# One attention, mixture and convolution program under a new table of step order and engine choices

## The chip, the cores and the metric

The kernel runs on one core of one Trainium2 chip. The metric is the device time of one execution in microseconds (us). Before the change the median of three runs is 481.59 us (481.58 to 484.25). A change of 1% is 4.8 us.

## The reference

Three blocks follow each other, for a batch of 4, a sequence of 448, 12 heads of 64 and a model width of 768:

```python
# 1. causal attention of 12 heads; x is its output, heads side by side: (4, 448, 768)
attn = softmax(mask(q @ k.T / 8));  x = attn @ v
# 2. four experts, each a causal attention head of its own; the two best by gate are mixed
logits = x @ w_gate
out += w_e * (softmax(mask((x @ wq[e]) @ (x @ wk[e]).T / 8)) @ (x @ wv[e]) @ wo[e])
# 3. feed-forward block: relu, a convolution of width 3 along the sequence, a sigmoid gate
h = relu(out @ w_in);  y = (h * sigmoid(conv3(h, conv_w))) @ w_out
```

All is computed to nearly full 32-bit accuracy. A matrix product is therefore done in three passes over operands that are split into a rounded high part and a remainder (`hi` and `lo` in the code).

## The kernel before, in words

The work is a list of tasks (`Program.add`), and each task has an engine or a choice of engines. A table in the source, `ORDER`, is a packed list of pairs (task, engine). `Program.run` walks through it and issues the tasks in that order, each on the engine named. So the table alone sets the order of the instructions on each engine's queue and decides, where there is a choice, which engine does a step. Nothing is decided at run time: an engine runs its own queue in order and waits at semaphores.

The stages, in the order of time:

- **Attention heads.** `A b_p` is the pair p of heads of batch b (24 pairs). For batches 1 to 3 the natural q and k (tile `nat`) are split into `sk_A` by `hi`, then `lo` for k and `lo` for q (lines 349, 347 or 353 for the high part on POOL, ACT or DVE; line 356 for the remainder on POOL or DVE). TensorE (PE) makes scores into one of three PSUM banks (line 673, or 630 for batch 0 without the split). DVE adds the mask and takes the row maximum (line 686, tiles `P_A` and `nm_A`), which also frees the bank for the next score. ACT takes the exponent (line 695), DVE the sum and its reciprocal (lines 703, 706, tile `r_A`), and one of ACT, POOL and DVE scales the rows (lines 347, 349, 353). PE transposes (line 726), ACT or DVE evacuates to `PT_A`, PE multiplies with v (line 797), and the result is split into `xT`.
- **Experts.** `M b_p` is the pair p of experts of batch b (8 pairs), with projections on PE at lines 991 and 1042 and the same softmax (`P_M`, `nm_M`).
- **Weights, woven into the first 300 us.** Weights arrive as 64-bit floats. `from_f64` turns them into 32-bit floats (`wm` for the input weight, `wom` for the output weight; ACT line 440, DVE lines 445 to 457), and `fold_piece` splits them into `whl` and multiplies them (line 918). `wout_convert` makes sums and differences of quarters of the output weight (tile `wom`, line 356) and splits each into `wohl`, `hi` on ACT or DVE and `lo` on POOL or DVE. These are stored to memory for the last stage.
- **Feed-forward.** Lines 1338 to 1369 make the hidden layer and its gate; line 1471 does the output product with a seven-product scheme over quarters; line 1517 adds the quarters up; the last stores end the kernel.

The functions that matter for the steps below are short:

```python
def copy(e, dst, src, scale=1.0, scale2=None):        # lines 345 to 353
    if e == "ACT": nc.scalar.activation(dst, src, AF.Copy, scale=scale)
    elif e == "POOL": nc.gpsimd.tensor_scalar(dst, src, ...)
    else: nc.vector.tensor_scalar(dst, src, ...)
def two(e, dst, a, b, op):                            # line 356
    (nc.gpsimd if e == "POOL" else nc.vector).tensor_tensor(dst, a, b, op)
th = add(either("whi", ...), 0, hi, need, take=[whl], ..., port=True)   # in wout_convert
tl = add(either("wlo", 0, of_two(n)), 0, lo, [th], ...)
```

A few small products of the identity matrix with itself (line 1587) are put in by `warm` where the table's planner saw PE idle for long.

Of the kernel before, what the change touches and what calls it, by code (L numbers as in the profile page):

```python
# [35 lines left out]
    "xry9H9wXnQ!RRci4JAe@k$R*J=|Lut9mou_3)O={fDmXr8bEd-zaWFC1nM*L0+~aNqXtm-NDxYnMxpSiUy09%@39}S&xwB^#t=K$m&75|3~C<r"
    "0rd&RMo%DS5O%B!8^T^8chSR`bMyiF4n2WcM6IF@P^YLHlmJaZYtR<78x5e7=!fVB=p*zg8i`rM%wrC)N7yam5s`{HM=?sT(5zB%sj_s3ctb>z"
    "Mlm?dBIXvAM}aUbj1VKocrnwM6XFJD2XjZ<$KXMim~QkSnhNSgvq3bJ0Tl*~p(oJ8Xbt8Y@dxG<+gjRQI#xPgDg;fG1~6t!0@H!%EA7K{VfKi}"
    "m_tk!Gk{^CKqMTgwWy=0yXX~Bh>C&kF(@nzi^C3-Qb|LlY*J_G9Pur2h1f?LBTbMDrM6OU=>iET&4LC<o1`VuEP5WjgqD#&SQhppT7;b@nMpFx"
    "5NVaPP1+~rNi>Rr!lo>iPM5BgZkB2(dXkvrAtgwCMIMR_tHow19i%SOBTy#@#zXT4i$;njiU3NkC_^Ih=sXXvj|cEBu)UxhZvZq58sPcJ0rD;B"  # L40
    "taPumjS?W4DPKxIm0pzIm$vfSc{z}P5~FlcdMQ_>Aj%a9MZr;Su=iL{5wa*ren1{0Z;|ul_ryOytDsBL83{rrkSSyiSwJQf@pxjMk~am?^X5Q9"
    "lw&f2+)sH)nIKP-H$gj~N90cOQ}Q@vfxJXsCGUfF$a&Bi=o$GEL@VMHiHa0Ox*|)Fy9mNp@MkH@l)phBFcORh5Ajwh<Gd}(HigD#^A|u=u$IpT"
    "i@{3p9{HTy$&2x3cmn=4`6n642bIk8R(Njycght-LDrHzC4D8WB|ym^_EkHMAK>4Bbl_acJZ00qV^5VHQ1<P4yM_FT_kp*{JK&x2@D5yw8Eodq"
    "`2!{GC9_2fMaxC&MK`<`<gKFJA~*Oa1yKT}DyXeg3>8PEJLuG}_ALJy|1n?e;8MTYukCksup?Y_$m=Yjm5i6%@`g%~j(m~V(N2w(%#_F-z0|!T"
    "R*9(OwCJMfJ?$0P&f_^!Me`+Ehuxtov6Qqs9y@M|?u$HBfXXQr6|a=YO7avf^@P&K|He}k_wYyfkm4L)S8Of5pk7n|qDiP>@Fd?;94}trZ_qx`"
    "X81ty5+7AeEr!sLw0`PpiJ3~H$!QxUG3s{7LCI-JkK;4#nd6q)ft$p2QV&aTv~2OiVm57<dR~&Fb{0P^?!w`VZ%UpOKQEpJ-<AN58Qf8E(!s$C"
    "@k_XQu!bg}1@Z0pC9s9|vUsX^ruc2~9Cd}dQv8Pc1~*PUrd`r{aF9|&shjqYwg!&lH^KPQwc;2!L(78O!5@lOaWUEp#wg>3;}^#d+7x4svCcm&"
    "4$wCE>(pJU48KP`q7LGQaXZDIi!X}1z`fvS;G1F{9zsXb?~5V0ZSZICDDH%6!SC=ls4jdr4T0;Sb>eAsHeEp9#61V^;4X1raG!Asx|<%LYw3fu"
    "G1>$TkE7w%=@;~CI+&5c579R12XqcDPw&MK;6*qEPKW!4W8Cp4<8RuGW8SgkSaTp4X8J81M?a>Y;cjrZI0&AAr{d@EQ}~zo=lG9~-x({6cZ~n$"
    "e_(tCTX8NNfJ@;J_-)4l1H!yu#Oc?J1^gm@n|{j}1Fz$E@%xS}y`P?EP?>nfF$2lOF~9Kt$-j2|bikZchM1vY9D!L(wDT8S-f`lPF@(%E`niM4"  # L50
# [1601 lines left out]
```

## Time and profile before

| | before |
|---|---|
| median of 3 runs | 481.59 us (481.58 to 484.25) |
| profiled execution, own time | 482.01 us |
| its span, first to last instruction | 480.2 us |
| PE busy | 471.0 us (98%) |
| DVE, ACT, POOL busy | 392.9, 347.4, 333.1 us |
| DMA | 93.26 MB, mean 194 GB/s |

The profiled execution has 1.8 us outside of the span and lies 0.42 us over the median of the runs. Busy times are unions of an engine's instructions. PE's matmuls are pipelined, so its busy share says that it rarely stood still, not that it ran at its peak. Each view is one execution on the one core.

### The profile page before, as it was taken

What the parts mean: (1) busy time and instruction counts of PE and PEld (TensorE: products, weight loads), DVE (VectorE), ACT (ScalarE), POOL (GpSimd) and SP (SyncE); (2) the same over time, 40 slices, a digit from 0 to 9 for tenths busy, and PEclk for the clock granted to TensorE, in tenths of its full rate; (3) what the DMA queues carried; (4) which work ended last, traced back from release to release, by engine and by line L of the source; (5) the groups of instructions that cost most, each with busy time, mean ns of one, the idle gap of its engine ahead of it and who ended that gap; (6) DMA issues with size and microseconds to landing.
All of it is one profiled execution on the core that took longest, in us unless ns stands there. A gap on an engine that the chain in (4) does not pass through costs nothing.

```text
span 480.2 us, 9966 instructions
## 1 busy us (share of the span) xinstructions
PE 471.0 (98%) x3114; PEld 398.9 (83%) x3114; DVE 392.9 (82%) x1155; ACT 347.4 (72%) x965; POOL 333.1 (69%) x475
## 2 busy tenths in 40 slices
PE   8999999999899999999999999999999999999997
PEld 6667898988679888878988877888789999999996
DVE  4999999999999798998889893287878887968482
ACT  5999999999788789987889994268987445422000
POOL 4697899799787989986879896117486485641530
PEclk9999999999899999999999999999999999999999
DMA  7693769986675986856884846616666783752122
GB/s 220 207 211 110 209 181 239 277 268 169 193 230 158 265 258 184 201 179 185 259 212 120 197 156 202 286 72 235 205 226 219 257 308 125 242 212 76 40 77 96
DMA packets 45846, 93.26 MB, mean 194 GB/s; under 512 B 4833, under 2 KB 27233, under 8 KB 45793
## 3 DMA queue, kind: packets, MB, share of 16 engines
q1 hardware_dynamic: 45360, 92.28, 63.4%
q8 instruction: 24, 0.39, 0.3%
q10 hardware_dynamic: 432, 0.34, 0.2%
q14 instruction: 30, 0.24, 0.2%
HBM read 60.72 MB, written 25.69 MB: 180 GB/s over the span
## 4 chain that ended last, share of the span: by engine, by line
PE 85%; DVE 6%; POOL 4%; ACT 3%; issue 1%; DMA 1%; POOLq 0%; DVEq 0%; ACTq 0%
PE bank L1471 21%; PE bank L991 11%; PE bank L797 11%; PE bank L726 10%; PE bank L673 10%; PE bank L1338 8%; PE bank L1042 7%; PE bank L918 3%; PE bank L630 2%; DVE P_A L686 2%; ACT P_A L695 2%; PE bank L1587 1%; POOL P_M L349 1%; DVE wohl L353 1%; DMA wset<-wohl 1%
## 5 line engine op out<-in xcount | busy, mean ns | idle before, releaser
L695 ACT ACTIVATE P_A<-P_A,nm_A 112x224 f32<-112x224 f32 (+3 forms) x192 | 99.4, 521 | 9.4 <-DVE nm_A L686 8.8
L686 DVE CUSTOM_DVE_ANT_0 P_A<-bank,mask 112x448 f32<-112x448 f32 (+3 forms) x192 | 79.6, 440 | 10.0 <-PE bank L630 5.4
L356 POOL TENSOR_TENSOR sk_A<-nat,sk_A 64x448 fp32r<-64x448 f32 (+1 forms) x67 | 77.5, 1158 | 4.6 <-ACT sk_A L347 0.6
L991 PE MATMUL bank<-xT,wqk 128*128 128x448 f32 x288 | 66.9, 372 | 0.0
L726 PE MATMUL bank<-ident,P_A 112*112 112x112 f32 x480 | 61.2, 264 | 1.4 <-ACT PT_A L347 0.7
L349 POOL TENSOR_SCALAR P_A<-P_A,r_A 112x112 f32<-112x112 f32 (+3 forms) x95 | 48.4, 523 | 11.3 <-DVE r_A L706 9.6
L726 PEld LDWEIGHTS bank<-ident,P_A 112*112 112x112 f32 x480 | 48.9, 135 | 8.2 <-POOL P_A L349 1.7
L991 PEld LDWEIGHTS bank<-xT,wqk 128*128 128x128 f32 x288 | 51.7, 188 | 3.9 <-DVE nm_A L686 0.2
L673 PE MATMUL bank<-sk_A 128*112 128x224 f32 (+3 forms) x288 | 51.9, 305 | 0.2 <-DVE nm_A L686 0.2
L1359 DVE SCALAR_TENSOR_TENSOR bank<-h,cw,bank 128x448 f32<-128x448 f32 x64 | 42.6, 686 | 8.9 <-ACT bank L1357 7.4
L797 PE MATMUL bank<-PT_A,v 112*64 112x448 f32 (+3 forms) x384 | 49.9, 404 | 0.0
L347 ACT ACTIVATE P_A<-P_A,r_A 112x224 f32<-112x224 f32 (+3 forms) x94 | 46.3, 522 | 2.9 <-DVE r_A L706 1.6
L1471 PE MATMUL bank<-up,ws 128*128 128x448 f32 x198 | 46.7, 367 | 0.0
L347 ACT ACTIVATE PT_A<-bank 112x336 f32<-112x336 f32 (+1 forms) x94 | 42.0, 472 | 5.2 <-PE bank L726 4.8
L797 PEld LDWEIGHTS bank<-PT_A,v 112*64 112x64 f32 x384 | 25.5, 136 | 23.1 <-issue 11.5
L1471 PE MATMUL bank<-us,ws 128*128 128x448 f32 x180 | 44.3, 366 | 0.0
L673 PEld LDWEIGHTS bank<-sk_A 128*112 128x112 f32 x288 | 40.6, 175 | 4.1 <-issue 0.4
L1042 PE MATMUL bank<-wvg,xT 128*112 128x260 f32 x288 | 43.5, 290 | 0.0
L1471 PEld LDWEIGHTS bank<-up,ws 128*128 128x128 f32 x198 | 37.2, 188 | 3.3
L1042 PEld LDWEIGHTS bank<-wvg,xT 128*112 128x112 f32 x288 | 36.8, 175 | 2.3 <-issue 1.1
L349 POOL TENSOR_SCALAR P_M<-P_M,r_M,g_w 112x336 f32<-112x336 f32 (+3 forms) x63 | 36.1, 584 | 3.0 <-ACT PT_A L347 1.3
L695 ACT ACTIVATION_READ_ACCUMULATOR P_A<-P_A,nm_A 112x1 f32 x192 | 36.8, 192 | 0.0
(181 smaller groups left out, 1053.5 us busy)
## 6 DMA issues: line engine op xcount, KB each, us to landing
nat<-in_qk_dram SPq DMA_DIRECT2D x72, 224.0 KB, 4.0
ws<-wset SPq DMA_DIRECT2D x7, 1536.0 KB, 8.9
wset<-wohl SPq DMA_DIRECT2D x18, 512.0 KB, 4.5
g<-g SPq DMA_DIRECT2D x32, 224.0 KB, 2.6
wraw<-in_w_in_dram SPq DMA_DIRECT2D x12, 512.0 KB, 4.9
woraw<-in_w_out_dram SPq DMA_DIRECT2D x12, 512.0 KB, 4.9
v<-in_v_dram SPq DMA_DIRECT2D x24, 224.0 KB, 4.8
out_dram<-osb_c SPq DMA_DIRECT2D x21, 224.0 KB, 2.0
```

Source lines behind the costliest of these rows:

```text
L347: nc.scalar.activation(dst, src, AF.Copy, scale=scale)
L349: nc.gpsimd.tensor_scalar(dst, src, scale, 1.0 if scale2 is None else scale2, ALU.mult, ALU.mult)
L356: (nc.gpsimd if e == "POOL" else nc.vector).tensor_tensor(dst, a, b, op)
L673: nc.tensor.matmul(sp[:CP], t[:, j.o[h], m * CP : (m + 1) * CP], t[:, j.o[h] + k, :w], start=(k == 2), stop=(k == 1),)
L686: nc.vector.tensor_tensor_reduce(rows(i), st["s", i][:CP, :w], mask[:, S - w :], -SCALE, 3.0e38, ALU.add, ALU.min, st["nm"][:, i : i + 1],)
L695: nc.scalar.activation(rows(i), rows(i), AF.Exp, bias=st["nm"][:, i : i + 1], scale=-1.0, accum_out=st["sm"][:, i, 0:1],)
L726: nc.tensor.transpose(pt[:CP, o : o + CP], rows(i)[:, kt * CP : (kt + 1) * CP], ident[:CP, :CP])
L797: nc.tensor.matmul(st["ov"][h * D : (h + 1) * D, kt * CP : S], j.v[:, kt, h, :], j.PT[h][:, col_base[kt] : col_base[kt] + S - kt * CP], st ...
L991: nc.tensor.matmul(st["ps"][:, :S], proj["wqk"][:, a, cc, w, p * P : (p + 1) * P], xT[b, cc][:, b2, :], start=(cc == 0 and (a, b2) == PASS ...
L1042: nc.tensor.matmul(st[i][:CP, :VW], xT[b, cc][:, a, i * CP : (i + 1) * CP], proj["wvg"][:, b2, cc, :], start=(cc == 0 and (a, b2) == PASSE ...
L1359: nc.vector.scalar_tensor_tensor(y, h, w, y, ALU.mult, ALU.add)
L1471: nc.tensor.matmul(ps(pb)[:, :S], wset[s][:, a, m, c2 * P : (c2 + 1) * P], unit(operands[q, c2, name][0])[:, b2], start=(c2 == 0 and (a, b ...
```

## The change

Only the table `ORDER` is another one. The tasks, what they need, their buffers, the banks and all other lines are the same. The table decodes to another order of the same tasks and to other engines for some of the steps that have a choice.

```diff
 ORDER = (
-    "c-jrt$4}b{gD_xMa0ORz1y^tdS8&DMxPpH!xPwh*B_LS|NLB(ep9Ew+2}oAL<Xwr9l_*&$kU3E103-(>IRKdhkUd~B2TBeBascwK1Y}nFzUQxa"
...
+    "c-jTQM@-v`V*p@J@B~lr&jUQc6Fk8ayzvB2@WeKGm4KuYkW>QlDgk+wfTR*8tpp^M7^xJKcVN5&kQ{*I0OTEj^nl4b0LdXh4vc>##;ert!@$_E"
...
 )
```

Counted over the two programs, the steps that went to other engines in the first 300 us are these:

| step | DVE | ACT | POOL |
|---|---|---|---|
| `wohl` hi, 128x512 | 13 to 8 | 5 to 10 | |
| `wohl` hi, 128x256 | 4 to 0 | 2 to 6 | |
| `whl` hi, 128x512 | 1 to 1 | 2 to 7 | 9 to 4 |
| `whl` lo, 128x512 | 0 to 3 | | 12 to 9 |
| `sk_A` hi, 128x896 | 1 to 3 | 17 to 10 | 18 to 23 |
| `sk_A` lo of k, 128x448 | 2 to 8 | | 34 to 28 |

PE has the same products; only the identity products of line 1587 go from 17 to 19. SP issues the same 293 instructions. Three places show how the queues differ.

**Place 1, DVE, near the scores of the expert pair `M` 0_1** (`P_M_1_1`, `nm_M_1_1`) and the last head pairs of batch 1 (`P_A_5_1`, `P_A_5_0`). `wohl_1_2` is a split of the output weight. Rows of line 686 are the row maxima. Before:

```order
L829 TENSOR_TENSOR xT_3_1838<-bank_65,xT_3_1838 128x448
L353 TENSOR_SCALAR wohl_1_2_1860<-wom_1_0_1660 128x512
L356 TENSOR_TENSOR wohl_1_2_1860<-wom_1_0_1660,wohl_1_2_1860 128x512
L686 ISA P_M_1_1_1865,nm_M_1_1_1866<-bank_62,mask 112x224
...
L686 ISA P_M_1_1_1865,nm_M_1_1_1866<-bank_62,mask 112x112
...
L686 ISA P_M_1_1_1865,nm_M_1_1_1866<-bank_61,mask 112x448
...
L703 TENSOR_REDUCE r_A_5_0_1814<-sm_94 112x4
L706 RECIPROCAL r_A_5_0_1814<-r_A_5_0_1814 112x4
```

Now:

```order
L686 ISA P_A_5_1_1769,nm_A_5_1_1770<-bank_61,mask 112x336
...
L353 TENSOR_SCALAR wohl_1_2_1838<-wom_1_0_1638 128x512
L686 ISA P_A_5_0_1823,nm_A_5_0_1824<-bank_62,mask 112x448
...
L356 TENSOR_TENSOR wohl_1_2_1838<-wom_1_0_1638,wohl_1_2_1838 128x512
L703 TENSOR_REDUCE r_A_5_1_1771<-sm_92 112x4
L686 ISA P_A_5_0_1823,nm_A_5_0_1824<-bank_65,mask 112x224
...
L686 ISA P_A_5_0_1823,nm_A_5_0_1824<-bank_65,mask 112x112
...
L706 RECIPROCAL r_A_5_1_1771<-r_A_5_1_1771 112x4
```

The split stands one head earlier now, between row maxima of `A` 1_5, and its two halves are no longer next to each other.

**Place 2, POOL at the same place.** The `wom_1_0<-wom_1_0` step makes what the split `wohl_1_2` reads, so DVE's split waits for it. Before:

```order
L356 TENSOR_TENSOR wom_1_0_1660<-wom_1_0_1660 128x256
L349 TENSOR_SCALAR P_A_5_1_1720<-P_A_5_1_1720,r_A_5_1_1722 112x448
L356 TENSOR_TENSOR sk_A_1_1703<-nat_1_1_1704,sk_A_1_1703 128x448
L356 TENSOR_TENSOR sk_A_1_1768<-nat_1_0_1769,sk_A_1_1768 128x448
L349 TENSOR_SCALAR P_A_5_0_1812<-P_A_5_0_1812,r_A_5_0_1814 112x112
```

Now:

```order
L356 TENSOR_TENSOR wom_1_0_1638<-wom_1_0_1638 128x256
L356 TENSOR_TENSOR sk_A_1_1726<-nat_1_1_1727,sk_A_1_1726 128x448
L349 TENSOR_SCALAR P_A_4_0_1670<-P_A_4_0_1670,r_A_4_0_1672 112x336
L349 TENSOR_SCALAR P_A_5_1_1769<-P_A_5_1_1769,r_A_5_1_1771 112x448
L356 TENSOR_TENSOR sk_A_1_1726<-nat_1_1_1727,sk_A_1_1726 64x448
```

Before, three steps stood between the `wom` step and the first step that needs something from DVE's queue behind the split (`r_A_5_0`); now two do (the next needs `r_A_5_1`).

**Place 3, DVE near the head pair `A` 3_0** (`sk_A_0`, batch 3). Before:

```order
L686 ISA P_A_4_0_2863,nm_A_4_0_2864<-bank_61,mask 112x448
...
L353 TENSOR_SCALAR sk_A_0_2881<-nat_0_1_2882 128x2x448
L356 TENSOR_TENSOR wohl_1_2_2855<-wom_1_0_2544,wohl_1_2_2855 128x512
L353 TENSOR_SCALAR oc_0_2895<-bank_66 128x448
L703 TENSOR_REDUCE r_A_4_1_2834<-sm_88 112x4
```

Now:

```order
L356 TENSOR_TENSOR sk_A_4_2845<-nat_4_0_2846,sk_A_4_2845 64x448
L353 TENSOR_SCALAR sk_A_0_2873<-nat_0_1_2874 128x2x448
L356 TENSOR_TENSOR sk_A_0_2873<-nat_0_1_2874,sk_A_0_2873 128x448
L353 TENSOR_SCALAR wohl_1_2_2882<-wom_1_0_2605 128x512
L703 TENSOR_REDUCE r_A_5_0_2771<-sm_94 112x4
```

DVE has four such splits in a row where it had two.

## Rows read from the trace of the kernel before

**Rows 1.** The page: span, busy time by engine, the chain by engine.

```profile
span 480.2 us, 9966 instructions
PE 471.0 (98%) x3114; PEld 398.9 (83%) x3114; DVE 392.9 (82%) x1155; ACT 347.4 (72%) x965; POOL 333.1 (69%) x475
PE 85%; DVE 6%; POOL 4%; ACT 3%; issue 1%; DMA 1%; POOLq 0%; DVEq 0%; ACTq 0%
```

**Rows 2.** Windows of the span: busy time (instructions) by engine, granted clock, DMA.

```profile
core 0: us, PE busy (x) PEld busy (x) DVE busy (x) ACT busy (x) POOL busy (x), PEclk, DMA share, GB/s
12.00:120.00 108.00, 106.92 (x810) 86.50 (x812) 103.24 (x367) 105.49 (x321) 93.01 (x128) 1.00 0.75 208
120.00:132.00 12.00, 9.79 (x68) 7.52 (x65) 11.71 (x27) 8.80 (x25) 9.22 (x12) 0.86 0.65 192
132.00:288.00 156.00, 155.43 (x1176) 131.55 (x1175) 139.35 (x467) 137.25 (x411) 131.92 (x178) 1.00 0.71 200
288.00:420.00 132.00, 131.69 (x733) 113.73 (x732) 97.16 (x201) 80.53 (x176) 74.24 (x124) 1.00 0.62 216
```

**Rows 3.** Timeline around the stall: start, duration, engine, idle before and releaser.

```profile
123.85 0.65 POOL L349 TENSOR_SCALAR P_A<-P_A,r_A 112x448 f32<-112x448 f32 x1
123.91 3.05 DVE L353 TENSOR_SCALAR wohl<-wom 128x512 fp32r<-128x512 f32 x1 [0.22 <-POOL wom L356]
123.93 2.11 PE L797 MATMUL bank<-PT_M,vm 112*64 112x448 f32 x16
124.45 2.23 POOL L356 TENSOR_TENSOR sk_A<-nat,sk_A 128x448 fp32r<-128x448 f32 x2
127.60 0.38 DVE L686 CUSTOM_DVE_ANT_0 P_M<-bank,mask 112x224 f32<-112x224 f32 x1
127.77 0.67 ACT L440 ACTIVATE wm<-wraw 128x512 f32<-128x512 f32 x1 [2.69 <-issue]
128.24 0.90 PE L673 MATMUL bank<-sk_M 128*112 128x336 f32 x2 [2.21 <-DVE nm_M L686]
129.12 0.36 POOL L349 TENSOR_SCALAR P_A<-P_A,r_A 112x112 f32<-112x112 f32 x1 [2.44 <-DVE r_A L706]
```

**Rows 4.** Windows right behind the stall, columns as in rows 2.

```profile
128.30:130.00 1.70, 1.70 (x8) 1.50 (x9) 1.67 (x8) 1.70 (x6) 0.80 (x2) 0.50 0.83 269
130.00:132.00 2.00, 2.00 (x12) 1.79 (x11) 2.00 (x5) 2.00 (x6) 1.90 (x3) 0.59 0.97 271
```

**Rows 5.** Groups of one form: count, busy us, mean ns, idle before.

```profile
L353 DVE TENSOR_SCALAR wohl<-wom 128x512 fp32r<-128x512 f32 x13 | 10.6, 813 | 1.4 <-DMA wset<-wohl 1.2 <-POOL wom L356 0.2
L356 DVE TENSOR_TENSOR sk_A<-nat,sk_A 128x448 fp32r<-128x448 f32 x2 | 3.7, 1838 | 0.0
L356 DVE TENSOR_TENSOR sk_A<-nat,sk_A 64x448 fp32r<-64x448 f32 x3 | 2.0, 670 | 0.1
L356 POOL TENSOR_TENSOR sk_A<-nat,sk_A 128x448 fp32r<-128x448 f32 x34 | 39.2, 1155 | 2.0 <-ACT sk_A L347 0.6
L349 POOL TENSOR_SCALAR P_A<-P_A,r_A 112x336 f32<-112x336 f32 x23 | 14.0, 610 | 3.9 <-DVE r_A L706 3.4 <-DVE r_A L703 0.2
```

**Rows 6.** Timeline of one split that meets POOL and one that does not.

```profile
151.89 1.15 POOL L356 TENSOR_TENSOR sk_A<-nat,sk_A 64x448 fp32r<-64x448 f32 x1
151.93 1.59 DVE L356 TENSOR_TENSOR sk_A<-nat,sk_A 128x448 fp32r<-128x448 f32 x1
154.29 0.41 DVE L353 TENSOR_SCALAR wohl<-wom 128x512 fp32r<-128x512 f32 x1
155.79 0.74 POOL L356 TENSOR_TENSOR wom<-wom,wom 128x256 f32<-128x256 f32 x1 [2.74 <-DVE wohl L356]
```

**Rows 7.** Timeline of PE: transposes, scores, identity products.

```profile
120.74 1.12 PE L726 MATMUL bank<-ident,P_A 112*112 112x112 f32 x10
121.63 1.24 PE L673 MATMUL bank<-sk_M 128*112 128x448 f32 x6
5.50 2.27 PE L1587 MATMUL bank<-ident 128*128 128x128 f32 x18
```

More of the change, by code (lines that the diff above doesn't have):

```diff
@@ L36 @@
[L36 to L50, printed above, removed]
@@ L96 @@
[L96 to L98 removed]
+    "c-jTQM@-v`V*p@J@B~lr&jUQc6Fk8ayzvB2@WeKGm4KuYkW>QlDgk+wfTR*8tpp^M7^xJKcVN5&kQ{*I0OTEj^nl4b0LdXh4vc>##;ert!@$_E"
+    "Zdfl24;R9~@E6#Z*h%aYY%dl8&%oMY6!;*P1e3$GFh48;yM*1qOfU!R81@798a@wSf^Wlj;e)Ud*fi`V>@DmStgm38fCcX;5WpR91zZQWz}MiX"
+    "@C$ezegxly-@+#gK49svkJu&HDr^(B4cmw1VW0wJ0lr|mpsPSyFj6p95P(PFZSWp=AG`z3E!2aIpx+VVLM19!uvoBOATQJwiVA22oC0luvEZ`M"
@@ new lines @@
+    "Rp2Y|7e)#*g|UK6L3^RO&{c>>bQe+(gN4I|H-){0V8r_Z1mbhSmx9BB<ASq-yMl{?&)6Zj6O=8SEPP+cLhupGg=>gS#0Xr5&>*G@L4`g<9&v=o"
+    "!rv8c7H$>p7akOjAp4L5$T8$e;c4LxViGxxJVjg};s`gwf@nkZAchcqhy?Zl_91p3VMe{dzQf)ka>xZF5{W~CkRyl;svWh8+&~^70VE5lK)!)n"
+    "kXy)h#4hpx=|bVr-6$9c0Rp2D=nrUAA-)hO44`5t8Cr)FAzes6@(g)_yhEZ;U{o)Pg&sr=qkbjEke$d3vKyI2;ZZy2ee@}sf>xvXXcO9rp2Un`"
+    "CQ!HNafB7?z+Rvu=owTFwSrnl9inrXW$ZKJbK*<l2^zqxViqt=3<xuZnZ`^aW)MgW4nr^Hl!{9KKu}RElmL}Rx1*O)pHcg$6Vxe6fRSOYP`9Xc"
+    "%mFHh#e>?4e3(t*Ht~?SjoHIo5s{=@Vi4Vf9zu_!htW8a1JjE>!u-G-U_hi};tyhHk)pJ%biA~`6acY69i;-$E^!jwQ<N*6ES)a3V04%mrW2FF"
@@ new lines @@
+    "^keq1{YBlFK}=Vv9u)#bK-ZW%3<`_G4wep=g0TRJMN*Uaq=ix`={0eV_>Q<t>?h5W#z}*uVG<R)Ncuq3mp%e*khVycQg>;vl!cunWk4p<EINn&"
+    "gcf2K(W|8!rBbX0yH!f1xF{Kli!@F0kyc1CQWuCt@l*Jep`y{EPExi=PT3=AC@?OXOXSkHF0P;3&mH8pQ;d{hZWn2?$U_d2rJx8UPx?Vhl>Px)"
+    "0UcsbuxHqBrC&=kBrccF&2lHWeV{?m2q+8crhF-laIdgurFW$$3YgMI8KbmuJGeN?9Tr>^CqE#MlPAf@qD^w1yiFz)-IKnNu1OFwf_zcB0h%W-"
+    "lD9#7pkWHNh(Kl+vB`Y0g8Pc{j515naUr}%<j3R*&@_1t^pyOJEaz!>P9BoCL=hHIdGaD{5sQ}xb#YfHGu#~aGnYb^la0K;K_D;^Y%FpX;lTiy"
+    "1wI0ugM7RkWs{;I&x2egZ6*Gaj*?yS73e4Bnu6mUkwstyc!hjQz9gH-_mnNl0(XVG&fVvpaQVC_FT;DtyC*||KddX(4XYOXl-FNEECH2lTlcKl"
@@ L99 @@
+    "B!9-*l2ftHWP7kX_-pLf;Oo$ziM`lgv7TgqayGdU$H!T5S=^X#CZ^-L_-+!28{?UTCZ0>~#=pi*F;5KDN@%6FvRh|jzsC-f?zpzq+}f2GNC;Y$"
+    "t=EbB#M6W*4o%{c$mB`#EP0h&YaLA9CSk3v*3H(=)}Gd#)`tmZvcGk_HPDJmO|{Op0?BCWFRe%M^SCH^(t6f9-#XMPPia%n6XujF<%>Uvcf=Q4"
+    "qw!ekIu1?T#*vAU)@<Uc^{%xoMM#aOCKH{h{Z?60lk7=>Q+=u5QadSXik;d|9i~oFUGb;!?YJ@NPUc(vsngUyQd6nflpr;qT1<UNO()(Zd`Vma"
+    "NXXOL^nUs<ZBDz=3yJrMlk`UFHswzz((&Y3`ZE1@x-C7Po=VTA=hNT}BGZ}fN%yBAX+j2-re+q?8|e>ec7~ANN>kH==@)5XW+cT*i_@}<DdWiK"
+    "Gye}Cay~W"
 )
```

102 lines of the change are left out of this document (50 added, 52 removed).

## The prediction

> **What bounds the kernel now.** I read the page first: of a span of 480.2 us PE is busy for 471.0, and 85% of the chain that ended last is PE [rows 1]. The reader is to see that a new order can't win much by making another engine faster; it wins where PE stands still or crawls. So the second view is the table of windows [rows 2]. PE's idle time is 108.00 - 106.92 = 1.08 us in 12 to 120, 2.21 us in 120 to 132, 0.57 us in 132 to 288 and 0.31 us in 288 to 420. One window of 12 us holds more than the 396 us around it, and it alone shows a granted clock below 1 (0.86).
>
> The third view is the timeline of that window [rows 3]. DVE starts the high part of a weight split (`wohl`, line 353) at 123.91 and is done 3.05 us later. The same form takes 0.41 us where POOL runs nothing [rows 6], and 0.81 us in the mean of 13 [rows 5]. POOL runs a 0.65 us step from 123.85 and two of `sk_A` until 124.45 + 2.23 = 126.68; only then does DVE move. Its next row maxima of `P_M` begin at 127.60. PE had a batch of line 797 of 2.11 us from 123.93 to spend, then waits 2.21 us for exactly that DVE line (row of 128.24: released by DVE `nm_M`, line 686). POOL's later wait of 2.44 us and ACT's of 2.69 us end with the same release, so nobody was the next in line: all engines lost the time together. That is why I take it to be real loss and not a wait that covers another. After it the clock is granted at 0.50 and 0.59 in the next 1.70 and 2.00 us [rows 4], the lower level (1.2 GHz), right behind the pause.
>
> The other DVE splits show the same sort of meeting at smaller prices: 1.59 us for a remainder that began 0.04 us after a POOL step of 1.15 us [rows 6], and a mean of 1.84 us for the two of 128x448 against 0.67 us for the three of 64 partitions [rows 5]. None of these stopped PE for long, as the idle sums of the long windows say [rows 2].
>
> **The change, part by part.** Everything moves a little, so I cost the one place where PE lost time, then what is added, then the loads.
>
> *The stall goes from its place.* Now the split `wohl_1_2` stands on DVE between row maxima of `A` 1_5, its remainder one row maximum later, and the row maxima of `M` 0_1 follow well behind. What PE had lost is 2.21 us of idle [rows 3] and the slow clock: 1.70 x (1 - 0.50) + 2.00 x (1 - 0.59) = 0.85 + 0.82 = 1.67 us [rows 4]. Together -3.88 us.
>
> *It may come back smaller.* The split is still released by POOL's `wom` step, and POOL has two steps ready behind that one (`sk_A` of 1.16 us, `P_A` of 0.61 us, means of [rows 5]); the third needs a reciprocal that DVE makes behind the split. Taken as before, DVE would be held for up to 1.16 + 0.61 = 1.77 us instead of 126.68 - 123.91 = 2.77 us. What is late next is the row maximum of `A` 1_5_0 in bank 62, whose reader on PE comes after six transposes (six tenths of 1.12 us) and three scores of six matmuls (1.24 us), 1.9 us of cover [rows 7]. DVE's path from PE's last score is the split and the row maximum: 0.41 + 1.77 + some 0.6 = 2.8 us, the 0.6 estimated from the 0.38 us of a row maximum half as wide [rows 3]. The cost is between 0 (DVE comes when POOL is through) and 2.8 - 1.9 = 0.9 us. I take +0.5: the met remainder in rows 6 paid nearly all of POOL's step, so half of the full price is the middle, not the floor. Without a pause as long as 2.21 us I expect no slow clock; the shorter ones in the long windows have a granted clock of 1.00 [rows 2].
>
> *Two identity products more.* They are recorded as four; 18 took 2.27 us, so 0.50 us if PE had work, nothing if it was waiting [rows 7]. They stand where the planner sees PE idle: +0.2.
>
> *Loads.* DVE loses nine `wohl` halves and gains six `sk_A` remainders of k. At the met prices the six cost 6 x 1.84 = 11.0 us, at the unmet 6 x 0.67 = 4.0 us; the five large `wohl` alone gave back 5 x 0.81 = 4.1 us [rows 5]. So DVE is between even and 7 us heavier over the first 288 us, in which it is idle for 4.8 us in 12 to 120 and 16.7 us in 132 to 288 [rows 2]. POOL gives away six steps of 1.16 us (6.9 us), and more in its `whl` halves, and is idle for 15.0 us in 12 to 120. What POOL no longer does can't be met there. I cost the loads at 0 because PE is the bound, and their cover in 12 to 120 is thin on DVE (4.8 us) and on ACT (108.00 - 105.49 = 2.5 us): if it is gone, PE pays. In place 3 four splits stand in a row on DVE, but POOL's next steps wait for the last of them, so there is no step of POOL for it to meet. SP's loads and stores are the same in number; with DMA busy at 0.75 or less in the long windows [rows 2] I cost their new order at 0.
>
> By the Trainium skill, "SBUF — State Buffer", section "Who interferes with whom", DVE and GpSimd share a port pair as an exclusive lock, and whoever starts first holds it for the whole instruction while the other is blocked. By that rule alone the split would have been free when POOL's first step ended at 124.50, 0.59 us after it began. The trace disagrees in size: DVE stayed out over two more POOL steps, for 2.77 us. By the rule the return of the stall would cost at most 0.41 + 1.16 + 0.6 - 1.9 = 0.3 us, and the sum, with half of that in place of 0.5, would be 478.5 and not 478.8 us.
>
> *Sum.* The profiled execution's own time is 482.01 us, its span 480.2. 482.01 - 3.88 + 0.5 + 0.2 = 478.83. This execution lies 0.42 us over the median of the runs, so against 481.59 the forecast is **478.4 us**, 0.7% less.
>
> **The rivals.**
>
> *More comes back (faster by over 1%).* With all of POOL's relief and the new places, the small waits of PE go too: 3.88 + 1.08 + 0.57 + 0.31 = 5.84 us, no return and no extra products. 482.01 - 5.84 - 0.42 = 475.75 us. For it: those waits are mostly waits for the same three engines. Against it: a new order brings its own small waits, and the long windows were already at 99% and more. Chance 0.25.
>
> *The change doesn't do what it says: the stall only moves.* The split still follows POOL's `wom` step at once, and eight `wohl` halves of 128x512 and more `sk_A` steps are left on DVE. One stop of 3.88 us anywhere leaves 481.6 to 482 us. For it: the meeting in rows 6 shows that such meetings are common, and each needs only a second ready step of POOL to grow. Against it: only one meeting in 288 us grew to 3 us. Chance 0.18.
>
> *DVE's new splits hold up the row maxima (slower).* Three to four splits now stand in a row on DVE at three places of the attention stage, and six remainders of k came to DVE whose two kin took 1.84 us each. If POOL has two or more steps ready in each of these places, DVE is late by over the 2.11 us that a batch of line 797 covers; from there PE stops, and a stop with its slow clock cost 3.88 us. Three of them against the one that goes: 482.01 + 2 x 3.88 - 0.42 = 489.35 us. For it: the prices in rows 5. Against it: place 3 shows POOL waiting for DVE there. Chance 0.12.
>
> **How the numbers follow.** The forecast has the remaining 0.45, and its own range is 476.9 to 480.5: the return of the stall between 0 and 0.9 + 1.67 with the slow clock, the products between 0 and 0.5, and about 1 us for new small waits. The range that holds 8 in 10 takes in the faster rival to 474.5 and the moved stall to 484.5, and leaves out the slower rival and a little below. A change of 1%, 4.8 us, is about what a measurement of this kernel can tell from none. Faster by over 1% means under 476.8: the faster rival and a sliver of the forecast, 0.28. Slower means over 486.4: most of the slower rival, 0.10. Within 1%: 0.62.
>
> **What would show it.** In the changed profile no DVE step of line 353 or 356 before 300 us should last over 2.3 us, no window of 12 us between 12 and 288 should have over 1 us of PE idle, and the clock should be 1.00 in all of them. The split `wohl` near 125 us should show 0.4 to 2.2 us. POOL's busy time should be lower before 288 us, DVE's about the same. I am wrong if a PE wait of over 2 us for `nm_A` or `nm_M` stands elsewhere, if the clock falls again, or if PE's busy time itself grows in the long windows without a wait that stands out.

## The result: 0.9% slower, and the profile after

The changed kernel takes 486.52 us in the median of 4 runs (486.22 to 487.05), against 481.62 us for the kernel before. The ratio is 1.0092, with a 95% interval of 1.0071 to 1.0112. The forecast of 478.4 us has the wrong sign, and the range that was to hold 8 in 10, 474.5 to 484.5, ends 2 us too low. The profiled execution took 486.78 us, so the two traces are 486.78 - 482.01 = 4.77 us apart.

The first lines of the page after, which answer to [rows 1]: span, busy time by engine, and the shares of the chain that ended last.

```profile
span 484.9 us, 9943 instructions
PE 471.3 (97%) x3118; PEld 396.7 (82%) x3118; DVE 399.2 (82%) x1161; ACT 346.4 (71%) x971; POOL 324.5 (67%) x463
PE 61%; DVE 12%; POOL 10%; ACT 7%; DMA 4%; issue 4%; SPq 1%; DVEq 0%; POOLq 0%; ACTq 0%
```

PE's busy time is the same within 0.3 us, so PE was not given more work. But PE's share of the chain fell from 85% to 61%: the end now hangs on DVE, POOL, ACT and DMA as well. The windows, with the columns of [rows 2] and in answer to them, say where.

```profile
12.00:120.00 108.00, 105.18 (x799) 84.10 (x800) 100.53 (x356) 103.55 (x316) 94.96 (x130) 1.00 0.73 201
120.00:132.00 12.00, 11.12 (x91) 8.61 (x88) 11.36 (x40) 10.45 (x32) 9.26 (x11) 1.00 0.93 270
132.00:288.00 156.00, 152.78 (x1152) 129.72 (x1152) 136.04 (x464) 136.32 (x410) 118.05 (x165) 1.00 0.71 195
288.00:420.00 132.00, 130.44 (x730) 110.55 (x727) 104.00 (x210) 76.36 (x174) 69.13 (x119) 1.00 0.62 216
```

The stop in 120 to 132 is smaller, 0.88 us of PE idle for 2.21, and the granted clock there is 1.00 for 0.86. The three long windows, which had 1.96 us of PE idle together, have 2.82 + 3.22 + 1.56 = 7.60. What PE waits for, summed over the trace (columns: who waits, for whom, us in sum, times, longest):

```profile
PE bank L726 <- POOL P_M L349: 1.8, 2, 1.0
PE bank L726 <- DVE P_M L351: 1.4, 2, 0.9
PE bank L1587 <- POOL ident masks.py:199: 1.4, 1, 1.4
PE bank L726 <- DVE P_A L353: 1.1, 1, 1.1
PE bank L673 <- DVE nm_A L686: 0.9, 2, 0.5
PE bank L673 <- DMA sk_M<-sk_M: 0.8, 1, 0.8
PE bank L726 <- POOL P_A L349: 0.5, 1, 0.5
PE bank L1042 <- POOL wvg L356: 0.5, 1, 0.5
```

The row of 1.4 us for `ident` is the start of the kernel and is in both. The rest wait for POOL, DVE and a DMA queue, none over 1.1 us at a time (three more of 0.2 to 0.3 us are left out). Before, the same view had one wait of 2.2 us and nothing else over 0.5 us after the start.

Idle time alone leaves out matmuls that are drawn out. So I put the two traces side by side at equal matmul work: each TensorE step counts as long as steps of its kind take back to back (the lower quartile over both traces), the steps are summed in the order of their ends, and the moments are compared at which the two traces have done the same sum.

```
work done, us    before at    changed at    changed minus before
      70            86.2          86.4           +0.18
      80            96.4          98.0           +1.61
     100           116.9         118.9           +1.99
     110           131.9         131.2           -0.75
     180           206.0         206.1           +0.11
     200           227.6         229.5           +1.91
     290           322.8         324.3           +1.56
     300           332.7         336.1           +3.37
     350           385.7         389.7           +3.96
     370           405.8         410.3           +4.54
     end           476.6         481.2           +4.55
```

So 2.74 us were won at the old stop and 7.3 us lost elsewhere, net of 0.35 won in between. By the times of the kernel before, the losses are 0.2 before 86, 1.4 at 86 to 98, 0.4 up to 117, 0.9 over 132 to 206, 1.8 at 206 to 228, 1.8 at 323 to 333, and 0.6 twice at 333 to 406. Each trace is one execution; which of these sizes repeat is told behind the splices below.

Three of these stops in the timeline (start, duration, engine, instruction; in brackets the idle time before and what ended it). At 90, a short step in wait at the head of DVE's queue:

```profile
88.77 0.63 ACT L347 ACTIVATE wohl<-wom 128x512 fp32r<-128x512 f32 x1 [0.57 <-POOL wom L356]
90.10 0.37 ACT L347 ACTIVATE vm<-bank 112x256 f32<-112x256 f32 x1
90.50 0.16 DVE L1062 COPY lg<-bank 112x4 f32<-112x4 f32 x1 [1.31 <-ACT vm L347]
90.58 0.53 DVE L353 TENSOR_SCALAR P_A<-P_A,r_A 112x336 f32<-112x336 f32 x1
91.17 0.50 PE L726 MATMUL bank<-ident,P_A 112*112 112x112 f32 x3 [1.07 <-DVE P_A L353]
```

The reader is to follow this from the bottom up. PE waits for a normalisation that depends on nothing new; it stands behind the 0.16 us copy of the gate's logits, which waits for `vm` on ACT, which ran late behind a weight split that waited 0.57 us for POOL. At 212 to 220 it is POOL's queue:

```profile
212.16 0.94 POOL L349 TENSOR_SCALAR sk_A<-nat 128x896 fp32r<-128x896 f32 x1 [2.19 <-DMA nat<-in_qk_dram]
213.18 1.14 POOL L356 TENSOR_TENSOR sk_A<-nat,sk_A 128x448 fp32r<-128x448 f32 x1
214.31 2.23 POOL L349 TENSOR_SCALAR P_M<-P_M,r_M,g_w 112x448 f32<-112x448 f32 x4
216.60 1.07 PE L726 MATMUL bank<-ident,P_M 112*112 112x112 f32 x9 [0.85 <-POOL P_M L349]
217.88 2.25 POOL L349 TENSOR_SCALAR P_M<-P_M,r_M,g_w 112x224 f32<-112x224 f32 x4
220.18 0.59 PE L726 MATMUL bank<-ident,P_M 112*112 112x112 f32 x4 [0.96 <-POOL P_M L349]
```

POOL stood 2.19 us for a load, though the reciprocal that the first four normalisations need was done at 211.25, and then ran two steps of the loaded tile's split ahead of them. At 331 to 335 it is a port meeting of a kind that no split takes part in on DVE's side:

```profile
331.59 3.70 DVE L351 TENSOR_SCALAR P_M<-P_M,r_M,g_w 112x224 f32<-112x224 f32 x3
331.69 0.53 POOL L349 TENSOR_SCALAR P_M<-P_M,r_M,g_w 112x112 f32<-112x112 f32 x1 [0.64 <-DVE r_M L706]
332.19 1.15 POOL L356 TENSOR_TENSOR ux<-ux 128x448 fp32r<-128x448 f32 x1
333.31 0.56 POOL L349 TENSOR_SCALAR ux<-ux 128x448 fp32r<-128x448 f32 x1
333.95 1.15 POOL L356 TENSOR_TENSOR ux<-ux 128x448 fp32r<-128x448 f32 x1
335.35 0.79 PE L726 MATMUL bank<-ident,P_M 112*112 112x112 f32 x6 [0.87 <-DVE P_M L351]
```

Three normalisations of the last batch's first expert pair (`M` 3_0), which POOL did before, now stand on DVE. The table's own charge for them is 0.34 + 0.42 + 0.38 = 1.14 us (260 + 0.36 per column, in ns, in the function `head`); they take 3.70 us beside POOL's splits of the FFN input `ux`.

### The profile page after: what moved, and what is told of

It is laid out like the page before. It is cut to its first block, busy times and chain, and to the rows that moved or that the text cites. A ratio compares the mean times of both kernels' runs of the same rounds, so it can differ in the third digit from the quotient of the medians.

```text
span 484.9 us, 9943 instructions
## 1 busy us (share of the span) xinstructions
PE 471.3 (97%) x3118; PEld 396.7 (82%) x3118; DVE 399.2 (82%) x1161; ACT 346.4 (71%) x971; POOL 324.5 (67%) x463
## 4 chain that ended last, share of the span: by engine, by line
PE 61%; DVE 12%; POOL 10%; ACT 7%; DMA 4%; issue 4%; SPq 1%; DVEq 0%; POOLq 0%; ACTq 0%
PE bank L1471 21%; PE bank L797 7%; PE bank L1338 7%; PE bank L726 7%; PE bank L673 6%; PE bank L991 6%; PE bank L1042 5%; ACT P_A L695 3%; POOL P_M L349 3%; POOL sk_A L356 2%; DVE P_A L686 2%; DMA sk_M<-sk_M 2%; PE bank L918 2%; PE bank L630 1%; DMA woraw<-in_w_out_dram 1%
## 5 line engine op out<-in xcount | busy, mean ns | idle before, releaser
L695 ACT ACTIVATE P_A<-P_A,nm_A 112x448 f32<-112x448 f32 (+3 forms) x192 | 99.7, 523 | 9.7 <-DVE nm_A L686 9.4
L356 POOL TENSOR_TENSOR sk_A<-nat,sk_A 64x448 fp32r<-64x448 f32 (+1 forms) x61 | 70.4, 1153 | 5.1 <-ACT sk_A L347 1.5
L349 POOL TENSOR_SCALAR P_A<-P_A,r_A 112x448 f32<-112x448 f32 (+3 forms) x89 | 44.1, 509 | 20.5 <-DVE r_A L706 10.1
L673 PE MATMUL bank<-sk_A 128*112 128x448 f32 (+3 forms) x288 | 51.7, 307 | 0.6 <-DVE nm_A L686 0.3
L347 ACT ACTIVATE P_A<-P_A,r_A 112x448 f32<-112x448 f32 (+3 forms) x95 | 46.6, 524 | 4.2 <-DVE r_A L706 3.6
L1471 PE MATMUL bank<-up,ws 128*128 128x448 f32 x207 | 49.0, 367 | 0.0
L347 ACT ACTIVATE PT_A<-bank 112x336 f32<-112x336 f32 (+1 forms) x91 | 40.9, 471 | 2.8 <-PE bank L726 2.6
L1471 PEld LDWEIGHTS bank<-up,ws 128*128 128x128 f32 x207 | 38.7, 188 | 3.9 <-POOL up L356 0.4
L1471 PE MATMUL bank<-us,ws 128*128 128x448 f32 x162 | 40.2, 368 | 0.2
L349 POOL TENSOR_SCALAR P_M<-P_M,r_M,g_w 112x112 f32<-112x112 f32 (+3 forms) x61 | 34.8, 582 | 8.1 <-ACT P_M L695 3.8
```

The costliest lines, as they stand in the source:

```text
L349: nc.gpsimd.tensor_scalar(dst, src, scale, 1.0 if scale2 is None else scale2, ALU.mult, ALU.mult)
L673: nc.tensor.matmul(sp[:CP], t[:, j.o[h], m * CP : (m + 1) * CP], t[:, j.o[h] + k, :w], start=(k == 2), stop=(k == 1),)
L695: nc.scalar.activation(rows(i), rows(i), AF.Exp, bias=st["nm"][:, i : i + 1], scale=-1.0, accum_out=st["sm"][:, i, 0:1],)
L1471: nc.tensor.matmul(ps(pb)[:, :S], wset[s][:, a, m, c2 * P : (c2 + 1) * P], unit(operands[q, c2, name][0])[:, b2], start=(c2 == 0 and (a, b ...
```

## Experiments

The theory: the new order takes the old stop away and puts other steps right behind their producers, so that each late producer makes a short stop of its own (the first theory in the expectations). Its rivals: the loss is port meetings and nothing else (A); time that one repair wins is lost again at the next late producer (B); the loss hangs on the state that the early part leaves (C); an order that is better by measured charges is not better on the chip (D); the changed engines are the loss and not the places (E).

All are edits of the table alone. "Ratio" is to the kernel before, measured beside it in the same comparison, with its 95% interval. Runs of one kernel spread over 1 to 6 us, so a ratio settles about 0.2%; what an edit did at its place is read from its trace. The expectations count a wait as the delay against matmuls back to back, some 0.2 us more than the idle time in the brackets of a row.

### The old stop, taken apart

The first edit takes only the step that the prediction named out of DVE's way, in the kernel before:

```diff
 ACT    P_A<-P_A,r_A 112x336
+ACT    wohl_1_2 hi 128x512
-DVE    wohl_1_2 hi 128x512
-DVE    wohl_1_2 lo 128x512
 DVE    row maxima of M 0_1 (three), sum and reciprocal of A 1_5
+DVE    wohl_1_2 lo 128x512
```

SP's store of this split moves back by one place with it.

> The kernel before with one change: the upper part of the weight split that DVE held at 123.9 for 3.05 us goes to ACT, and its lower part and its save stand behind the four row maxima of M0_1 and the sum and reciprocal after them; nothing else of the new table. If the stop of 2.21 us and the 1.67 us of slow clock hang on this one step, as the prediction says, the time falls by 3.4 to 3.9 us, to 477.7 to 478.2, with a granted clock of 1.00 from 10 us on. Rival: the row maxima were late for another reason, or the lower part meets POOL's subtractions just as long a few rows on; then the time stays within 1 us of 481.6.

Measured: 482.97 us, ratio 1.0001 (0.9988 to 1.0015). Nothing was won. In its trace the row maxima are on time, and PE stops all the same:

```profile
126.60 1.61 DVE L356 TENSOR_TENSOR wohl<-wom,wohl 128x512 fp32r<-128x512 f32 x1 [0.62 <-ACT wohl L347]
128.24 0.67 ACT L440 ACTIVATE wm<-wraw 128x512 f32<-128x512 f32 x1 [1.67 <-DVE wohl L356]
129.39 0.86 PE L726 MATMUL bank<-ident,P_A 112*112 112x112 f32 x7 [1.90 <-ACT PT_A L347]
```

ACT's square of line 440 writes a `wm` buffer that the lower part of this very split frees. It waits at the head of ACT's queue, and behind it stand the copies of transposes that PE needs next. This is the 2.69 us of ACT in [rows 3], which I had taken for a symptom. The next edit moves the square too, and the last one of the study moves it alone:

```diff
-ACT    wm<-wraw 128x512 (square, line 440)
 ACT    PT_A<-bank (three copies, A 1_4, h=0)
+ACT    wm<-wraw 128x512 (square, line 440)
```

> The kernel before with the edit of the first experiment and one more: on ACT the square of a weight that waits for the split's lower part (it frees the square's buffer) stands behind the three copies of transposes out of PSUM (A1_4, h=0), instead of ahead of them; the bit step on DVE that reads the square moves with it. If the stop at 126 to 130 hung on two waits at once, the row maxima on DVE and these copies behind the waiting square on ACT, the time now falls by 2.2 to 3.9 us, ratio 0.992 to 0.9955, with under 0.6 us of PE idle from 124 to 132. Rival: a third producer (the lower part on DVE, the loads) is as late, and the ratio stays over 0.998.

Measured: 480.20 us, ratio 0.9955 (0.9938 to 0.9972). Its window, with the columns of [rows 2]:

```profile
120.00:132.00 12.00, 11.20 (x91) 7.91 (x88) 11.25 (x33) 10.92 (x32) 10.70 (x13) 1.00 0.77 228
```

> The kernel before with the second half of the seventh experiment alone: on ACT the square that waits for the split stands behind the three copies of transposes out of PSUM; DVE keeps the split ahead of the row maxima, as before. With the first half alone nothing was won, with both 0.45 per cent. If two waits end at the same stop, the row maxima still hold TensorE to 128.2 us and this half alone gives nothing either: ratio 0.998 to 1.002. Rival: the square's place alone made the stop, and the split on DVE, which the prediction took for its cause, was never the bound: ratio 0.994 to 0.997.

Measured: 482.26 us, ratio 0.9998 (0.9981 to 1.0015). The row maxima hold PE again, now behind the split's lower part:

```profile
125.05 3.12 DVE L356 TENSOR_TENSOR wohl<-wom,wohl 128x512 fp32r<-128x512 f32 x1
125.40 2.21 POOL L356 TENSOR_TENSOR sk_A<-nat,sk_A 128x448 fp32r<-128x448 f32 x2
128.73 0.56 PE L673 MATMUL bank<-sk_M 128*112 128x336 f32 x2 [2.00 <-DVE nm_M L686]
```

One half gives 0.0%, the other 0.0%, both 0.45%: two chains held PE at the same place, and each hid the other. Both together are worth 0.0045 x 482.77 = 2.2 us by the ratio (482.77 is the kernel before beside it). PE's order is the same in both, so the profiled executions can be compared matmul for matmul: this one goes from 0.30 us behind at 118 to 2.47 ahead at 136, so 2.8 us are won at that place, of which 0.5 are lost again at 281. Of the 2.8, idle time is 2.21 - 0.80 = 1.4 us, since PE keeps 0.80 us of idle in that window, more than the 0.6 expected. The other 1.4 us are matmuls that are no longer drawn out, with the granted clock at 1.00 for 0.86. I had priced the stop at 2.21 + 1.67 = 3.88.

### Where the loss sits: two splices

The tables agree so far in what is done when that one can be cut and continued with the other.

```diff
 ORDER = table before, steps 1 to 1,070 (to 141 us)
-        table before, the rest
+        changed table, the rest
```

> A splice: the table of the kernel before up to about 141 us (1,070 steps), the changed table from there on; program and buffers are the same. Between the two profiled executions, at equal matmul work done, the changed kernel stands 0.87 us ahead at 142 us and 4.55 us behind at the end. First theory (many short stops, each in its own place, whatever came before): this kernel has the old stop at 124 to 132 and all the new stops behind 141, so it stands 5.4 us behind the kernel before, ratio 1.010 to 1.012, slower than either. Rival C (the loss hangs on the early part: the loads or the phase of the engines as the new first 141 us leave them): within 1.5 us of the kernel before.

Measured: 487.23 us, ratio 1.0102 (1.0074 to 1.0131). Its waits hold the old stop and the new ones in one list, each at its own size:

```profile
PE bank L673 <- DVE nm_M L686: 2.2, 1, 2.2
PE bank L726 <- POOL P_M L349: 1.8, 2, 0.9
PE bank L726 <- DVE P_M L351: 1.4, 2, 0.9
PE bank L673 <- DMA sk_M<-sk_M: 1.0, 1, 1.0
```

```diff
-ORDER = table before, the steps up to 306 us
+ORDER = changed table, steps 1 to 2,250 (to 306 us)
         table before, the rest
```

> The other splice: the changed table up to about 306 us (2,250 steps), the table of before from there on. At equal work the changed kernel stood 1.6 us behind there and 4.55 at the end; the stops at 334 (1.8 us), 386 and 402 (0.9 together) lie behind the seam. First theory: 1.6 us behind the kernel before, ratio 1.002 to 1.005, faster than the changed kernel by 2.5 to 3 us. Rival B (time that one stop leaves is lost again at the next late producer): 3 us or more behind, ratio over 1.006.

Measured: 484.26 us, ratio 1.0036 (1.0020 to 1.0052). Both ratios lie where the comparison at equal work puts them. The first interval is too wide to tell that splice from the changed kernel, but it rules out rival C, which allows 1.003: the loss is in the places, not in the state that the early part leaves. By the second median, what 306 us had lost was neither regained nor enlarged by the rest; its profiled execution, the fastest of 12, ends only 0.3 us behind that of the kernel before.

> The changed kernel as it is, on the chip of this comparison, as the measure for the other three: 1.009 of the kernel before by the comparison in which it was first timed (1.0071 to 1.0112). If the loss were one of that one chip or execution, it would come out within 0.3 per cent of the kernel before.

No edit here: the changed kernel measured 487.67 us beside the two splices, ratio 1.0107 (1.0083 to 1.0130). It overlaps the first ratio, so the loss is not that of one chip or one execution; below I take 1.009 to 1.011 as its place.

Its profiled execution is a second one of the same table, and shows which stops repeat. PE's waits at 91 (1.07 us in both), at 220 (0.96 and 0.98) and at 334 to 335 (1.39 in sum in both) do. Others do not: PE waits 1.41 us at 84 where the first execution had 0.21, behind ACT, which stands for a load; the wait for `sk_M` at 164 is 1.33 for 0.81, and the first of the two at 216 to 220 is 0.34 for 0.85.

```profile
83.28 0.67 ACT L440 ACTIVATE wom<-woraw 128x512 f32<-128x512 f32 x1 [1.96 <-DMA woraw<-in_w_out_dram]
```

In the first execution ACT's wait for this load was 0.76 us. So the size of a stop with a load in its chain differs here by up to 1.2 us between two executions of one kernel, and a single trace does not settle it.

### Single stops repaired in the changed kernel

```diff
-DVE    P_M<-P_M,r_M,g_w 112x224, 112x448, 112x336 (M 3_0, h=1, line 351)
+POOL   P_M<-P_M,r_M,g_w 112x224, 112x448, 112x336 (M 3_0, h=1, line 349)
```

> The changed kernel with one change: the three normalisations of M3_0, h=1, that the new table gave to DVE (331.6 to 335.3) stand on POOL again, where they stood before. First theory (the new table adds short stops, each with a producer of its own): the two waits of 0.73 and 1.08 us at 334 to 335 go and the time falls by 1.3 to 1.8 us, to 484.7 to 485.2. Rival A (the new loss is port meetings between DVE and POOL and nothing else, and this is the largest): the same here, but nothing from the two other edits sent with it. Rival B (a stop that goes comes back at the next late producer): 0 to 0.5 us.

Measured: 485.96 us, ratio 1.0071 (1.0056 to 1.0086), 1.0 to 1.7 us under the changed kernel by the two measures of it. In the trace the four take 2.27 us on POOL, PE has no wait behind them, and matmul for matmul 1.5 us are won on the changed kernel at that place.

```profile
334.23 2.27 POOL L349 TENSOR_SCALAR P_M<-P_M,r_M,g_w 112x224 f32<-112x224 f32 x4 [0.64 <-DVE r_M L706]
336.03 1.12 PE L726 MATMUL bank<-ident,P_M 112*112 112x112 f32 x7
```

The second repair:

```diff
+DVE    P_A<-P_A,r_A 112x336 (A 1_1, h=0)
 DVE    lg<-bank 112x4
-DVE    P_A<-P_A,r_A 112x336 (A 1_1, h=0)
```

> The changed kernel with one change: on DVE the normalisation of A1_1, h=0, 336 columns, stands ahead of the copy of the gate's logits, instead of behind it; that copy stood 1.31 us in wait for ACT, and the normalisation with it. First theory: the wait of 1.28 us before the transposes at 91 goes, the time falls by 0.9 to 1.3 us, to 485.2 to 485.6. Rival A (port meetings alone): the normalisation at 89.2 meets POOL's addition that begins at 89.28, and nothing or at most 0.3 us is won. Rival B (given back at the next late producer): 0 to 0.4 us.

Measured: 485.91 us, ratio 1.0073 (1.0054 to 1.0093). That is 0.9 to 1.6 us by the ratios, but at its place the trace shows only 0.45 us. The wait of 1.07 is gone. The logits' copy still waits, 1.01 us now, and the row maxima behind it hold PE half a microsecond later:

```profile
89.55 0.39 DVE L353 TENSOR_SCALAR P_A<-P_A,r_A 112x336 f32<-112x336 f32 x1
90.94 0.16 DVE L1062 COPY lg<-bank 112x4 f32<-112x4 f32 x1 [1.01 <-ACT vm L347]
91.66 0.56 PE L673 MATMUL bank<-sk_M 128*112 128x336 f32 x2 [0.44 <-DVE nm_A L686]
```

By the ratios alone neither of these two repairs is clear of the changed kernel's interval (1.0071 to 1.0112); it is the traces that place their gains.

The third:

```diff
+POOL   P_M<-P_M,r_M,g_w (four, M 1_1, h=1)
 POOL   sk_A<-nat 128x896, sk_A<-nat,sk_A 128x448 (A 3_1, h=1)
-POOL   P_M<-P_M,r_M,g_w (four, M 1_1, h=1)
```

> The changed kernel with one change: on POOL the four normalisations of M1_1, h=1, stand ahead of the upper and lower part of A3_1 that waited for a load until 212.16 us, as in the kernel before. No DVE step was stretched there. First theory: the wait of 1.06 us at 216.6 goes, and part of it comes back since the split of A3_1 is later; the time falls by 0.4 to 1.1 us, to 485.4 to 486.1. Rival A (port meetings alone): no change. Rival B (given back at once): no change, or up to 0.5 us more.

Measured: 488.08 us, ratio 1.0114 (1.0097 to 1.0131): nothing won. In the trace the first wait is gone and 1.3 us are won by 217 us, of which the second wait (1.34 for 0.96) and the later split of A 3_1 take back 0.6 by 224:

```profile
212.15 2.25 POOL L349 TENSOR_SCALAR P_M<-P_M,r_M,g_w 112x448 f32<-112x448 f32 x4 [1.61 <-DVE r_M L706]
217.87 2.25 POOL L349 TENSOR_SCALAR P_M<-P_M,r_M,g_w 112x224 f32<-112x224 f32 x4
220.18 0.59 PE L726 MATMUL bank<-ident,P_M 112*112 112x112 f32 x4 [1.34 <-POOL P_M L349]
```

POOL's second four end at 220.1 in both kernels, since POOL has the same steps to do up to that moment. So about half is given back at once, as rival B has it, and the runs show no gain at all. Nor is all of the 1.3 us the edit's: without it, the first wait is 0.85 and 0.34 us in the two executions of the changed kernel, and it is absent in the trace of the second splice, which has the same table there. Rival A, port meetings and nothing else, falls: the stops at 90 and 216 have no DVE step in them that a meeting drew out as at 334, and still make 3 of the 7.3 us at equal work.

```diff
 (the first two repairs)
-PE     scores of M 1_0, h=0, 448 columns
 PE     transposes of A 2_2, h=1 (three groups)
+PE     scores of M 1_0, h=0, 448 columns
```

> The changed kernel with three local repairs at once: the normalisations of M3_0 back on POOL (second experiment), the normalisation of A1_1 ahead of the logits' copy on DVE (third), and on PE the first scores of M1_0, h=0, which waited 1.03 us for a copy of sk_M by DMA at 164, behind the three groups of transposes of A2_2 that came next. First theory (the stops add, each with its own producer): 1.7 us and 1.6 us as the two gave alone and 0.8 us more, so 4.1 us under the changed kernel, ratio to the kernel before 1.000 to 1.004. Rival B (what one repair gives is taken back at the next late producer): 1.005 or more.

Measured: 485.70 us, ratio 1.0051 (1.0032 to 1.0070), 2.0 to 2.7 us under the changed kernel, not 4.1. Against the changed kernel 0.5 us are won at 91 and 1.5 at 334. At 164 the wait for `sk_M` is gone from the list of waits, but nothing is won there: the transposes that were put ahead now wait themselves, for a normalisation on POOL.

```profile
165.18 1.39 PE L726 MATMUL bank<-ident,P_A 112*112 112x112 f32 x10 [0.68 <-POOL P_A L349]
```

So two of the three stops add, and the third was worth nothing: the first theory for the two, and for the third something near rival B, one wait for another.

### Orders of our own

```diff
-ORDER = table before
+ORDER = the search's: against the table before, 348 of 894 choices of engine and many places differ
```

> A table of our own, program and buffers the same. It was found from the table of the seventh experiment by moving steps and changing engines, with each step charged what the two traces show for it (medians by engine and shape), 0.6 us for a DVE step that meets POOL, and each candidate counted four times: as charged, with 40 ns more on every step off PE, with loads 1.2 us later, and with 120 ns more per hand-off between engines. First theory (what the changed table lost is the slack between producer and consumer): an order that keeps slack has fewer and shorter stops than either and beats the kernel before by 0.6 per cent or more, 474 to 480 us, ratio 0.983 to 0.994. Rival D (what an order gains on paper is lost on the chip whatever the charges, through loads and port meetings that no charge describes): 0.997 or more.

Measured: 484.42 us (483.02 to 489.15), ratio 1.0039 (1.0018 to 1.0061). This is in rival D's range; its reason is shown in part.

```profile
PE bank L673 <- DMA sk_M<-sk_M: 3.3, 2, 2.4
PE bank L630 <- DMA sk_A<-in_qk_dram: 1.7, 2, 1.1
```

Five microseconds of the profiled execution are waits for DMA, which the search charged at a fixed rate and latency. But that execution took 489.15 us, the slowest of 12 and 4.7 us over their median, so what the others lost is not shown.

```diff
-ORDER = changed table
+ORDER = the search's: against the changed table, 350 of 894 choices of engine and many places differ
```

> The same search begun from the changed table instead, which it keeps in half of its choices of engine or more. First theory: slack can be put back into the changed table as well as into the one of before; ratio 0.985 to 0.997. Rival E (the changed choices of engine themselves are the loss, not the places of the steps): 1.003 or more, with DVE or ACT late at many places.

Measured: 488.45 us, ratio 1.0116 (1.0093 to 1.0139), with waits of PE for DVE and ACT, at nine places and of 0.2 to 1.4 us each. Two orders made with durations read from these traces are slower than the kernel before. So the first theory fails where I stretched it to a remedy: charges read from the traces did not bring slack that lasts on the chip. Rival E is left open by this, since its condition was met but the search moved places as well.

## Why the prediction was wrong

**"Nobody was the next in line: all engines lost the time together."** Wrong in mechanism. The three waits did not end with one release: ACT's ended at 127.77, behind the split's lower part, PE's at 128.24 behind the row maxima, POOL's at 129.12 behind a reciprocal. ACT's was a chain of its own, through a buffer, and the three edits show it: each half alone gives nothing, both give 0.45%. This cost the forecast little, since the changed table relieves both chains. The place gave back 2.74 us at equal work, where the first two terms have 3.88 - 0.5 = 3.38. The slow clock was priced a little high: 2.74 less the idle time won, 2.21 - 0.88, leaves 1.4 us for 1.67.

**"It may come back smaller", +0.5.** Right in mechanism and size. The split lasted 1.19 us, inside the 0.4 to 2.2 forecast, and PE then waited 0.54 us for a row maximum of the head pair; the other 0.34 us of idle in the window came before the split began.

```profile
123.17 1.19 DVE L353 TENSOR_SCALAR wohl<-wom 128x512 fp32r<-128x512 f32 x1
124.96 0.66 PE L673 MATMUL bank<-sk_M 128*112 128x448 f32 x2 [0.54 <-DVE nm_A L686]
```

**"Two identity products more", +0.2.** The trace has four matmul records more, as counted; they were not tried alone.

**"Loads at 0", and "about 1 us for new small waits".** This is the step that failed. The loads and new waits stand in the sum at nothing and in the range at 1 us; they cost 7.3 us at equal work. The profiled execution missed its sum by 486.78 - 478.83 = 7.95 us, of which these are 7.3 and the old place 0.64. The term did not fail by the price that I named: the eight remainders of 128x448 on DVE took 693 ns in the mean, not 1838, and the `wohl` halves 518 ns for 813. Nor was DVE even to 7 us heavier: it was 6.4 us less busy over 12 to 288 us, though the prediction's list leaves out three `whl` remainders and two `sk_A` upper parts that came to it.

```profile
L353 DVE TENSOR_SCALAR wohl<-wom 128x512 fp32r<-128x512 f32 x8 | 4.1, 518 | 0.7 <-POOL wom L356 0.7
L356 DVE TENSOR_TENSOR sk_A<-nat,sk_A 128x448 fp32r<-128x448 f32 x8 | 5.5, 693 | 0.8 <-POOL sk_A L349 0.7
L351 DVE TENSOR_SCALAR P_M<-P_M,r_M,g_w 112x448 f32<-112x448 f32 x1 | 2.2, 2202 | 0.0
```

Before 300 us the change eased the meetings: summed over DVE steps that ran at least 0.12 us past the lower three tenths of their shape, the time over it fell by 6 to 7 us. After 300 us it rose by as much, and the two long normalisations of line 351 (2.20 and 1.25 us, charged 0.42 and 0.38) come on top. The sum counts every stretched step, whether or not POOL was the cause. The prediction weighs no step of DVE or POOL behind 300 us.

What I missed is in [rows 2]. PE idle of 1.08, 0.57 and 0.31 us means that the old order has hardly a late producer in 396 us, with DVE and ACT idle for 2 to 5 us in 108. I read the thin cover and wrote that PE pays if it is gone, and priced it at 0. A new order of 3,114 steps with 346 of 894 choices of engine changed sets each hand-over between engines anew, and has no more than 1.96 us to win there. Each place with a new stop cost 0.4 to 1.8 us at equal work. That the thin cover is why so many hand-overs came late is argued and not shown: the two orders that were to put slack back came out slower.

**The range.** The forecast's own range, 476.9 to 480.5, does not come out of the terms that it names: without return, products and small waits they give 477.7, with all of them 481.8. The time lies outside of either.

**SP's order, 0.** Also too low. Six loads of `nat` issued in 196 to 212 us took 6.6 us to land in the median, against 4.8 before, and PE waited 0.8 us for a copy of `sk_M` at 164.

**The slower rival, 0.12.** Right in sign, wrong in mechanism and price. PE waits for row maxima at 122 and 125 alone, 0.9 us in all. The stops come from POOL's queue, a copy at the head of DVE's queue that waits for ACT, DVE's normalisations and a DMA, without a slow clock (1.00 in all four windows), at a fraction of 3.88 us each.

**What would show it.** No step of lines 353 or 356 before 300 us over 2.3 us, no PE wait over 2 us, clock 1.00, POOL's busy time lower before 288 us: these came true. One did not: two windows of 12 us have over 1 us of PE idle, 1.07 in 84 to 96 and 1.56 in 216 to 228. None of the three signs of being wrong appeared. Signs made for one large wait do not see many small ones. The sum of idle time over the long windows does.

**What stays open.** The 0.9 us over 132 to 206, the 0.4 us at 98 to 117 and the two of 0.6 us behind 333 were not tried one by one; the repair at 164 gave nothing. How much of the 7.3 us belongs to loads that land at other times in each execution is open too. Which account of loads and meetings would let a search find an order as good as the one before is not settled: two tries failed.

## What to carry to other kernels

Where the bound engine is idle for 2 us in 400, a reordered schedule has little to win and much to lose: price it by the hand-overs that it sets anew, here 0.4 to 1.8 us for each late one, and not by the one stop that it removes. All three reordered tables here came out slower than the one before. Before a stop is booked as a gain, look for a second wait that ends with the first; if each alone gives nothing, they must go together. Read a stop's size from two executions before it is repaired, if a load stands in its chain. The best version here is the small one: the old table with one split and one square moved, 480.20 us, ratio 0.9955 to the kernel before, faster than both.
